# Turning 33 of 36 activation tiles by VectorE blocks and a DMA round trip instead of on TensorE

## The chip, the cores and the metric

The kernel runs on one core of one Trainium2 chip. The metric is the device time of one execution in microseconds (us). A core has five engines that run side by side, each in its own program order: TensorE (PE in the profile, with PEld for its weight loads), VectorE (DVE), ScalarE (ACT), GpSimd (POOL) and SyncE (SP), which here issues the DMA transfers. Engines hand work to each other by semaphores. TensorE writes to PSUM, all others work mostly in SBUF, and large arrays lie in HBM.

## The reference

First comes an attention with a feature map instead of a softmax: 8 batches, 8 heads, 576 positions, 64 channels. Then comes a gated feed-forward layer over the 4608 tokens, with 512 channels outside and 1024 inside.

```python
def phi(x):                       # 64 -> 2 x 128 features
    proj = x @ w_phi
    proj = proj - max(abs(proj), axis=-1)
    return concatenate([exp(proj), exp(-proj)], axis=-1)
q_p, k_p = phi(q), phi(k)
attn = (q_p @ (k_p.T @ v)) / (q_p @ sum(k_p, axis=seq) + 1e-6)
x = attn as (4608, 512)
h = x @ w_in                      # (4608, 1024)
sm = exp(h - max(h)) / (sum(exp(h - max(h))) + 1e-9)
solu = h * sm
ln = (solu - mean(solu)) / sqrt(var(solu) + 1e-6) * g_ln
out = ln @ w_out                  # (4608, 512)
```

All of it is float32. The kernel keeps that accuracy by splitting operands into a high and a low part and adding three products (high by high, high by low, low by high).

## The kernel before

**The work in pieces.** The attention runs over 16 units `u`, each a batch and half of its heads, in two halves `sub`. Keys are projected in five groups (`kp`), then reduced to their maximum, subtracted and exponentiated; a "visit" `V` sums the keys' features with the values on TensorE (`kvT`), and from the seventh visit on it also contains the previous half's numerators and denominators (`num`, `den`). Denominators go through a DMA that spreads them (`ds`, `db`). From unit 2 on, the sums `kv` are turned by VectorE in blocks of 32 by 32 (`kv_turn`), written to HBM (`kv_out`) and read back in four pieces (`kv_in`), which the plan names `kve`, `kvo` and `kvi`.

The feed-forward layer runs over 36 tiles `t` of 128 tokens, interleaved with the attention as their inputs come ready. For one tile: `moe_hi` and `moe_lo` split the input; `moe_h` multiplies it with `w_in` in two halves of 12 matmuls into a PSUM tile `h` of 128 by 1024; `moe_max`, `moe_exp` and `moe_u` on VectorE, ScalarE and VectorE make the gated activation `eu`; `moe_var` and `moe_scale` its scale; `moe_t` (line 1176) transposes `eu` on TensorE in two groups of four 128 by 128 blocks into a PSUM tile `uT`; `moe_uh` (line 1183) on ScalarE and `moe_ul` (line 1189) on VectorE split each group into the high part `uh` and the low part `ul`; `moe_o` (line 1193) multiplies these with `w_out` in two halves of 12 matmuls; `moe_oe` scales and `moe_od` stores.

**Buffers.** `SBUF_BUFS` (line 43) gives the number of buffers of each kind. `big` is a kind of 4 KB per partition: `eu`, `uh` and `ul` of a tile each take one, and the weights' preparation takes some at the start. `mo` is a pair of PSUM banks that `uT` and `o` share up to tile 30.

**The order.** Each piece is entered with `op(...)` into a `Plan`: engine, an estimated cost, what it comes after, which buffers it takes and which tiles it uses. `prioritize` (line 197) gives each piece a priority from two tables of numbers, and `order` (line 212) plays the plan through with the estimated costs and takes, on each engine, the piece that can start and has the best priority. The pieces are then issued in that order, and each engine keeps it: a piece that has to wait holds all behind it on the same engine. This includes SP, where a transfer that waits for its data holds the later ones. Every instruction is recorded through one helper (line 345), so groups in the profile are told apart by their tiles' names, not by their lines.

Of the kernel before, what the change touches and what calls it, by code (L numbers as in the profile page):

```python
# [8 lines left out]
F32 = mybir.dt.float32  # L9
# [11 lines left out]
P = 128  # L21
# [4 lines left out]
SWITCH, STICK, LINGER = 165.0, 400.0, 330.0  # L26
TILED = dict(visit=(1, 2), q_num=(1, 1), q_den=(2, 2))
# [4 lines left out]
JOIN, OWN = 6, 4  # L32
PORT = (
    "w_bits", "w_in_lo", "w_sum", "w_center", "w_out_lo", "k_lo", "z_add", "q_lo", "q_sub", "divide", "moe_lo",
)
# [4 lines left out]
TAIL_T = 31  # L40

# [3 lines left out]
    xa=1, xb=1, m2k=5, big=3, nm=2, sm=3, bst=2, mv=2, sa=2, sc=3,  # L45
# [5 lines left out]
WINDOW = 10240 / 3  # L51
START = dict(tensor=0.0, vector=950.0, scalar=4000.0, gpsimd=1750.0, sync=600.0)
LATENCY = {
    ("tensor", "vector"): 200, ("tensor", "scalar"): 200, ("scalar", "tensor"): 270, ("scalar", "vector"): 130,
    ("scalar", "gpsimd"): 160, ("vector", "tensor"): 260, ("vector", "scalar"): 130, ("vector", "gpsimd"): 200,
    ("gpsimd", "tensor"): 310, ("gpsimd", "scalar"): 120, ("gpsimd", "vector"): 150, ("vector", "vector"): 127,
    ("scalar", "scalar"): 143, ("gpsimd", "gpsimd"): 100, ("tensor", "tensor"): 60,
}

BASE = (
# [4 lines left out]
)  # L67
OFFSET = (
# [47 lines left out]
)  # L116


def act(n, psum=False, operands=0):
    return n / 1.2 + (51 if psum else 93) + 93 * operands  # L120


def dve(n):
    return (n + 65) / 0.96

# [16 lines left out]

class Plan:


    def __init__(self, bufs):
        self.ops, self.index, self.bufs = [], {}, dict(bufs)

    def op(self, name, engine, cost, prio, fn, args=(), after=(), alloc=(), tiles=(), early=None):
# [5 lines left out]
                 port=fn.__name__ in PORT, early=early or {})  # L155
        )

    @staticmethod
    def lat(a, b):
        if a == "start":  # L160
            return 0.0
# [1139 lines left out]
```

## Time and profile before

| | before |
|---|---|
| three runs | 774.5, 776.04, 776.7 us; median 776.04 |
| span of the profiled execution | 771.7 us (the profile shows no time outside of its span) |
| TensorE busy | 747.6 us, 97% of the span, 4935 matmuls |
| VectorE, ScalarE, GpSimd busy | 498.0, 384.1, 471.0 us |
| DMA | 75.35 MB in 99968 packets |

The span goes from the first to the last instruction. A run's time contains a little more than that, so a span is compared with a span and a median with a median. A row of a group reads: line, engine, operation, what it writes from what it reads, shapes, count, then busy us in total, mean ns of one, and the idle time of that engine just before, with what ended it. A row of the chain of waits reads: start us, duration us, engine or queue, tile, count; each piece is what released the next.

### The profile page before, as it was taken

Reading aid. Unit: us, or ns where it says so; the run is one execution under the profiler, and the core shown is the slowest. Engines: PE = TensorE matmul, PEld = TensorE weight load, DVE = VectorE, ACT = ScalarE, POOL = GpSimd, SP = SyncE. Lnnn points to the kernel's source line nnn. Section 1 sums busy time; section 2 is a strip of 40 time slices with the busy share of each in tenths; the row PEclk is TensorE's granted clock in tenths of the full one; section 3 lists DMA queues with packets and bytes.
Section 4 is the critical chain, followed back from the end, with each engine's and each line's share of the span. In section 5 each row is a group of like instructions: output and inputs, shape, how many; then the busy total and the mean of one; then the engine's idle time right before and its main releaser. Section 6 shows DMA issues by size and latency. Waiting matters only on the chain.

```text
span 771.7 us, 13472 instructions
## 1 busy us (share of the span) xinstructions
PE 747.6 (97%) x4935; PEld 564.6 (73%) x4935; DVE 498.0 (65%) x861; ACT 384.1 (50%) x750; POOL 471.0 (61%) x507
## 2 busy tenths in 40 slices
PE   5889999999999999999999999999999999999997
PEld 3566577777776777777777777778777777788885
DVE  4987896867568575766767658568377574435342
ACT  3776665465545455555546455545446354223221
POOL 1154799688957768694959786946849573422110
PEclk8899999999999999999999999999999999999999
DMA  7754432344333142524343433423323212110000
GB/s 237 291 177 134 110 106 66 92 135 139 84 111 94 54 128 75 136 75 120 104 110 113 132 92 98 122 67 101 84 71 102 68 35 62 40 44 27 14 24 31
DMA packets 99968, 75.35 MB, mean 98 GB/s; under 512 B 56128, under 2 KB 90432, under 8 KB 99392
## 3 DMA queue, kind: packets, MB, share of 16 engines
q1 hardware_dynamic: 99904, 74.50, 33.2%
q8 instruction: 39, 0.64, 0.3%
q14 instruction: 25, 0.20, 0.1%
HBM read 59.38 MB, written 15.09 MB: 96 GB/s over the span
## 4 chain that ended last, share of the span: by engine, by line
PE 93%; DVE 3%; DMA 1%; ACT 1%; SPq 1%; issue 1%; POOL 0%; ACTq 0%; POOLq 0%
PE o L345 26%; PE h L345 26%; PE kvT L345 11%; PE num L345 8%; PE pjk L345 6%; PE uT L345 4%; PE den L345 4%; PE pq L345 4%; DVE w L345 1%; PE pjq L345 1%; PE dT L345 1%; SPq L345 1%; DMA rawk<-in_k 1%; DVE cmp L345 0%; DVE m L345 0%
## 5 line engine op out<-in xcount | busy, mean ns | idle before, releaser
L345 PE MATMUL o<-w_out_h,uh 128*128 128x512 f32 x288 | 115.7, 402 | 0.5 <-DVE ul L345 0.5
L345 PE MATMUL o<-w_out_l,uh 128*128 128x512 f32 x288 | 114.1, 396 | 0.0
L345 PE MATMUL o<-w_out_h,ul 128*128 128x512 f32 x288 | 114.0, 396 | 0.0
L345 POOL TENSOR_TENSOR zacc<-zacc,ek 128x512 f32<-128x512 f32 (+1 forms) x78 | 100.7, 1291 | 19.2 <-ACT ek L345 13.3
L345 ACT ACTIVATE ek<-dk 128x512 f32<-128x512 f32 (+1 forms) x160 | 88.4, 582 | 42.9 <-DVE dk L345 42.6
L345 PE MATMUL h<-win_h,mxh 128*128 128x512 f32 x288 | 92.9, 404 | 0.0
L345 PE MATMUL h<-win_h,mxl 128*128 128x512 f32 x288 | 90.7, 396 | 0.0
L345 PE MATMUL h<-win_l,mxh 128*128 128x512 f32 x288 | 90.7, 396 | 0.0
L345 DVE TENSOR_REDUCE nm<-h 128x1 f32<-128x1024 f32 x36 | 43.9, 1220 | 63.4 <-PE h L345 63.3
L345 ACT ACTIVATE fq<-pT 128x576 f32<-128x576 f32 x104 | 68.9, 677 | 28.2 <-DVE pT L345 12.3
L345 ACT CAST uh<-uT 128x512 fp32r<-128x512 f32 x72 | 41.4, 585 | 83.6 <-PE uT L345 56.3
L345 POOL TENSOR_TENSOR blk<-blk,mcol 128x1152 f32<-128x1152 f32 x26 | 55.5, 2135 | 36.5 <-ACT mcol L345 36.3
L345 ACT ACTIVATE eu<-h,nm 128x1024 f32<-128x1024 f32 x36 | 40.2, 1117 | 68.9 <-DVE nm L345 62.1
L345 POOL TENSOR_TENSOR hq<-rawq,hq 64x1152 fp32r<-64x1152 f32 x26 | 69.1, 2658 | 7.2 <-ACT hq L345 4.9
L345 DVE TENSOR_TENSOR ul<-uT,uh 128x512 fp32r<-128x512 f32 x72 | 47.9, 676 | 37.4 <-ACT uh L345 37.3
L345 PE MATMUL num<-fq,kvf 128*64 128x288 f32 x512 | 69.3, 412 | 0.0
L345 DVE TENSOR_REDUCE m<-pjk 128x4 f32<-128x512 f32 (+1 forms) x80 | 48.8, 626 | 27.1 <-PE pjk L345 26.6
L345 PE MATMUL kvT<-ek,rawv 128*64 128x256 f32 x512 | 64.5, 383 | 1.7 <-ACT ek L345 1.7
L345 DVE TENSOR_TENSOR eu<-h,eu 128x1024 f32<-128x1024 f32 x36 | 43.9, 1218 | 34.0 <-ACT eu L345 34.0
L345 PEld LDWEIGHTS h<-win_h,mxl 128*128 128x128 f32 x288 | 54.3, 189 | 13.1
L345 PEld LDWEIGHTS o<-w_out_h,ul 128*128 128x128 f32 x288 | 54.2, 188 | 13.2
L345 PEld LDWEIGHTS h<-win_l,mxh 128*128 128x128 f32 x288 | 54.2, 188 | 13.1
(107 smaller groups left out, 1568.2 us busy)
## 6 DMA issues: line engine op xcount, KB each, us to landing
rawq<-in_q SPq DMA_DIRECT2D x26, 576.0 KB, 4.3
rb<-d SPq DMA_DIRECT2D x64, 144.0 KB, 3.3
out<-os SPq DMA_DIRECT2D x36, 256.0 KB, 2.0
rawk<-in_k SPq DMA_DIRECT2D x64, 128.0 KB, 2.8
rawv<-in_v SPq DMA_DIRECT2D x64, 128.0 KB, 2.3
dk<-kvs SPq DMA_DIRECT2D x28, 192.0 KB, 1.9
kvf<-dk SPq DMA_DIRECT2D x112, 48.0 KB, 2.5
wraw<-in_w_in SPq DMA_DIRECT2D x4, 1024.0 KB, 5.7
```

What stands on the lines that cost most here:

```text
L345: return self.tc.keep_in_program_order(method(*args, **kwargs))
```

## The change

Tiles 0 to 32 (`TURN_PE = 33`) no longer use `moe_t`. VectorE turns `eu` in 32 by 32 blocks into a buffer `B` (`moe_turn`); SP writes `B` to HBM in one transfer of 512 KB (`moe_bout`) and reads it back in four of 128 KB, one for each quarter of the partitions (`moe_bin`), so that features stand on partitions; ScalarE makes the high part in one copy of 1024 columns (`moe_uhs`) and VectorE the low part in one subtraction (`moe_uls`), both from SBUF. Tiles 33, 34 and 35 keep the old way.

There are eight `big` buffers instead of three; a changed tile takes five over its life (`eu`, `B`, `uT`, `uh`, `ul`). All eight prepared pieces of weights use `big`, where the last one used another kind. The two tables of priorities and the planner that plays the plan through are gone. In their place stands `SEQUENCE`, one table with the place of each of the 2827 pieces, and `order` only walks through it and hands out buffers. The relative order of the pieces that both kernels have differs too: on TensorE 65 of 474 common pieces stand at the same place among them, and none is moved by more than 19 places. The SBUF reserved for DMA descriptors that software writes is set to 2048 bytes.

```diff
+TURN_PE = 33
-    xa=1, xb=1, m2k=5, big=3, nm=2, sm=3, bst=2, mv=2, sa=2, sc=3,
+    xa=1, xb=1, m2k=5, big=8, nm=2, sm=3, bst=2, mv=2, sa=2, sc=3,
...
-BASE = (
...
-OFFSET = (
...
+SEQUENCE = (
+    3, 95, 0, 2, 136, 102, 132, 7, 97, 105, 140, 98, 133, 99, 88, 89, 106, 103, 107, 137, 117, 134, 135, 8, 144,
...
     def order(self):
...
+        for i in SEQUENCE:
+            o = self.ops[i]
+            assert written.issuperset(o["after"]), o["name"]
+            written.add(o["name"])
             for tag, t in o["alloc"]:
+                slot[t] = free[tag].pop(0)
+            for t in tiles[i]:
+                pending[t] -= 1
+                if not pending[t]:
+                    free[tag_of[t]].append(slot[t])
+        return [self.ops[i] for i in SEQUENCE]
...
-    w_tag = ("big", "big", "big", "big", "big", "big", "big", "e")
+    w_tag = ("big",) * 8
...
+    def moe_turn(t):
+        M["B", t] = sb("big", [P, 4, 8, 32], name="ub")
+        nc.vector.transpose(
+            out=M["B", t].rearrange("p b k j -> p k b j"),
+            in_=M["e", t].rearrange("p (k b i) -> p k b i", k=8, b=4),
+        )
+
+    def moe_bout(t):
+        M["du", t] = dram.tile([P, 4, 256], F32, tag="du", name="du", bufs=40)
+        nc.sync.dma_start(out=M["du", t], in_=M["B", t].rearrange("p b k j -> p b (k j)"))
+
+    def moe_bin(t, b):
+        if b == 0:
+            M["uT", t] = sb("big", [P, 4, 8, 32], name="uTs")
+        src = M["du", t].rearrange("(a i) b x -> i a b x", a=4)
+        nc.sync.dma_start(
+            out=M["uT", t][32 * b : 32 * b + 32].rearrange("p a k j -> p a (k j)"), in_=src[:, :, b, :]
+        )
+
+    def moe_uhs(t):
+        M["uh", t] = sb("big", [P, 8, P], F32R, "uhs")
+        M["turned", t] = M["uT", t].rearrange("p a k j -> p k a j")
+        nc.scalar.copy(out=M["uh", t].rearrange("p k (a j) -> p k a j", a=4), in_=M["turned", t])
+
+    def moe_uls(t):
+        M["ul", t] = sb("big", [P, 8, P], F32R, "uls")
+        full, hi, lo = M["turned", t], M["uh", t], M["ul", t]
+        hi, lo = (x.rearrange("p k (a j) -> p k a j", a=4) for x in (hi, lo))
+        hi_lo_sub(nc.vector, lo, full, hi)
+
...
-        for i in range(2):
+        by_dma = t < TURN_PE
+        if by_dma:
+            op(n("tb"), "vector", 1265, z + 8, moe_turn, (t,), [n("u")], [("big", n("B"))], [n("e")])
+            op(n("bo"), "sync", dma(4 * P * DF), z + 9, moe_bout, (t,), [n("tb")], (), [n("B")])
+            for b in range(4):
+                op(n("bi", b), "sync", (560, 440), z + 9.5, moe_bin, (t, b), [n("bi", b - 1) if b else n("bo")],
+                   () if b else [("big", n("uT"))], [n("uT")])
+            op(n("uh", 0), "scalar", act(DF), z + 11, moe_uhs, (t,), [n("bi", b) for b in range(4)],
+               [("big", n("uh"))], [n("uT")])
+            op(n("ul", 0), "vector", dve(DF), z + 12, moe_uls, (t,), [n("uh", 0)], [("big", n("ul"))], [n("uT"), n("uh")])
+        for i in range(0 if by_dma else 2):
...
-               [n("ul", hf)] + ([n("o", 0)] if hf else [("wol", f) for f in range(8)]),
+               [n("ul", 0 if by_dma else hf)] + ([n("o", 0)] if hf else [("wol", f) for f in range(8)]),
...
-    nc = bacc.Bacc("TRN2", target_bir_lowering=False, num_devices=1)
+    nc = bacc.Bacc("TRN2", target_bir_lowering=False, num_devices=1, dynamic_dma_scratch_size=2048)
```

More of the change, by code (lines that the diff above doesn't have):

```diff
@@ L25 @@
 EPS = 1e-6
-SWITCH, STICK, LINGER = 165.0, 400.0, 330.0
-TILED = dict(visit=(1, 2), q_num=(1, 1), q_den=(2, 2))
 K_PLAIN = (0, 1, 2)
@@ L31 @@
 KV_PE = (0, 1)
[L32 to L35, printed above, removed]
+SWITCH = 165.0
+JOIN = 6
 PJ_TAGS = ("mo", "h", "mo", "mo", "h")
@@ L49 @@
 NVZ = 2
[L51 to L58, printed above, removed]
-BASE = (
[4 rows of a table removed]
-)
-OFFSET = (
[47 rows of a table removed]
+SEQUENCE = (
[148 rows of a table added]
 )
@@ L153, in op @@
             dict(name=name, engine=engine, cost=cost, prio=prio, fn=fn, args=args, after=list(after),
-                 alloc=list(alloc), tiles=list(tiles), mode=TILED.get(fn.__name__, (0, 0)),
-                 port=fn.__name__ in PORT, early=early or {})
-        )
[L158 to L161, printed above, removed]
-        if a == "sync":
-            return 1150.0 if b == "tensor" else 910.0
-        return LATENCY.get((a, b), 150.0)
-    def dep_lat(self, a, b):
-        if a["engine"] == b["engine"] == "sync" and a["name"][:2] == b["name"][:2]:
-            return -1e9
-        return self.lat(a["engine"], b["engine"]) - a["early"].get(b["name"], 0.0)
@@ L171, in pe_end @@
-    @staticmethod
-    def pe_end(columns, t, cost):
-        rest = 2.4 * cost
-        while rest > 1e-6:
-            w = int(t / WINDOW)
-            rate = 2.4 if columns.get(w - 1, 0.0) >= 3060 else 1.2
-            n = min(rest, rate * ((w + 1) * WINDOW - t) + 1e-6)
-            columns[w] = columns.get(w, 0.0) + n
-            rest -= n
-            t += n / rate
-        return t
-    @staticmethod
-    def promote(ops, left, done, queue, head, free, ready):
-        def fits(i):
-            tags = [tag for tag, _ in ops[i]["alloc"]]
-            return tags and all(len(free[tag]) >= tags.count(tag) for tag in tags)
-        waiting = [i for e in ENGINES for i in ready[e] if fits(i)]
-        i = min(waiting, key=lambda i: (ops[i]["prio"], i))
-        for tag in {tag for tag, _ in ops[i]["alloc"]}:
-            rest = queue[tag][head[tag] :]
-            queue[tag][head[tag] :] = [x for x in rest if x[1] == i] + [x for x in rest if x[1] != i]
@@ L197, in prioritize @@
-    def prioritize(self):
-        groups, kinds = {}, {}
-        for o in self.ops:
-            group, kind = self.place(o["name"])
-            o["prio"] = BASE[groups.setdefault(group, len(groups))] + OFFSET[kinds.setdefault(kind, len(kinds))]
-    @staticmethod
-    def place(name):
-        if isinstance(name, str) or isinstance(name[0], str) and name[0] != "moe":
-            return "w", (name, "")
-        if name[0] == "moe":
-            return name[:2], ("moe", *name[2:])
-        return name[0], (name[1:], min(name[0], OWN))
@@ L212, in order @@
-    def order(self):
-        ops = self.ops
-        n = len(ops)
-        preds = [[self.index[a] for a in o["after"]] for o in ops]
-        succs = [[] for _ in range(n)]
-        for i, p in enumerate(preds):
-            for a in p:
-                succs[a].append(i)
-        left = [len(p) for p in preds]
-        users, tag_of = {}, {}
-        for i, o in enumerate(ops):
-            for tag, t in o["alloc"]:
-                tag_of[t] = tag
-            for t in set(o["tiles"]) | {t for _, t in o["alloc"]}:
-                users.setdefault(t, []).append(i)
-        pending = {t: len(u) for t, u in users.items()}
-        tile_end = {}
-        free = {tag: [(0.0, "start", k) for k in range(c)] for tag, c in self.bufs.items()}
-        slot = {}
-        queue = {tag: [] for tag in self.bufs}
-        for i, o in enumerate(ops):
-            for tag, t in o["alloc"]:
-                queue[tag].append((o["prio"], i, t))
-        for q in queue.values():
-            q.sort()
-        head = {tag: 0 for tag in self.bufs}
-        engine_free = dict(START)
-        done = [None] * n
-        ready = {e: [] for e in ENGINES}
-        for i in range(n):
-            if not left[i]:
-                ready[ops[i]["engine"]].append(i)
-        sequence = []
-        dma_free = 0.0
-        dma_done = [0.0] * 8
-        columns = {}
-        mode = 0
-        port = {"vector": (-1.0, -1), "gpsimd": (-1.0, -1)}
-        while len(sequence) < n:
-            best = None
-            for e in ENGINES:
-                cand = []
-                for i in ready[e]:
-                    t = engine_free[e]
-                    if e == "sync":
-                        t = max(t, dma_done[-8] + 910.0)
-                    for a in preds[i]:
-                        t = max(t, done[a] + self.dep_lat(ops[a], ops[i]))
-                    ok = True
-                    want = {}
-                    for tag, _ in ops[i]["alloc"]:
-                        want[tag] = want.get(tag, 0) + 1
-                    for tag, k in want.items():
-                        h = head[tag]
-                        mine = [x[1] for x in queue[tag][h : h + k]]
-                        if mine != [i] * k or len(free[tag]) < k:
-                            ok = False
-                            break
-                        f = sorted(free[tag])[k - 1]
-                        t = max(t, f[0] + self.lat(f[1], e))
-                    if ok:
-                        cand.append((t, ops[i]["prio"], i))
-                if not cand:
-                    continue
-                t0 = min(c[0] for c in cand)
-                same = lambda i: e != "tensor" or ops[i]["mode"][0] == mode
-                lim = max(t0, engine_free[e]) + 1e-6
-                pick = min(
-                    (c for c in cand if c[0] <= lim + (LINGER if e == "tensor" and 0 < ops[c[2]]["mode"][0] == mode else 0)),
-                    key=lambda c: (c[1] + (0 if same(c[2]) else STICK), c[2]),
-                )
-                if best is None or (pick[0], pick[1]) < (best[0], best[1]):
-                    best = (pick[0], pick[1], pick[2], e)
-            if best is None:
-                self.promote(ops, left, done, queue, head, free, ready)
-                continue
-            t, _, i, e = best
-            o = ops[i]
-            for tag, tl in o["alloc"]:
-                f = min(free[tag])
-                free[tag].remove(f)
-                slot[tl] = f[2]
-                head[tag] += 1
-            if e == "sync":
-                hold, transfer = o["cost"]
-                hold += 180 if len(dma_done) < 15 else 40 if len(dma_done) < 22 else 0
-                engine_free[e] = t + hold
-                dma_free = done[i] = max(t + hold + 625, dma_free) + transfer
-                dma_done.append(done[i])
-            elif e == "tensor":
-                engine_free[e] = done[i] = self.pe_end(columns, t, o["cost"] + SWITCH * (o["mode"][0] != mode))
-                mode = o["mode"][1]
-            else:
-                end = t + o["cost"]
-                if o["port"]:
-                    other = "gpsimd" if e == "vector" else "vector"
-                    busy, j = port[other]
-                    shared = min(o["cost"], max(0.0, busy - t))
-                    if shared > 0:
-                        end += shared
-                        engine_free[other] += shared
-                        done[j] += shared
-                        port[other] = (busy + shared, j)
-                    port[e] = (end, i)
-                engine_free[e] = done[i] = end
-            ready[e].remove(i)
-            sequence.append((t, i))
-            for s_ in succs[i]:
-                left[s_] -= 1
-                if not left[s_]:
-                    ready[ops[s_]["engine"]].append(s_)
-            for tl in set(o["tiles"]) | {x for _, x in o["alloc"]}:
-                pending[tl] -= 1
-                prev = tile_end.get(tl, (0.0, e))
-                tile_end[tl] = max(prev, (done[i], e))
-                if not pending[tl]:
-                    free[tag_of[tl]].append((*tile_end[tl], slot[tl]))
-        self.slot = slot
-        self.length = max(done)
-        self.start = {ops[i]["name"]: t for t, i in sequence}
-        return [ops[i] for _, i in sequence]
@@ new lines, in op @@
+                 alloc=list(alloc), tiles=list(tiles), early=early or {})
+        )
+    def order(self):
+        assert sorted(SEQUENCE) == list(range(len(self.ops)))
+        tiles = [list(dict.fromkeys([*o["tiles"], *(t for _, t in o["alloc"])])) for o in self.ops]
+        tag_of = {t: tag for o in self.ops for tag, t in o["alloc"]}
+        pending = {}
+        for t in (t for ts in tiles for t in ts):
+            pending[t] = pending.get(t, 0) + 1
+        free = {tag: list(range(c)) for tag, c in self.bufs.items()}
+        self.slot = slot = {}
+        written = set()
+        for i in SEQUENCE:
+            o = self.ops[i]
+            assert written.issuperset(o["after"]), o["name"]
+            written.add(o["name"])
+            for tag, t in o["alloc"]:
+                slot[t] = free[tag].pop(0)
[4 more added lines that the diff above has]
+        return [self.ops[i] for i in SEQUENCE]
@@ L1254, in linear_attention_then_moe @@
         op(n("od"), "sync", dma(4 * P * DM), z + 19, moe_od, (t,), [n("oe")], (), [n("os")])
-    plan.prioritize()
     for o in plan.order():
```

198 rows, old and new, of tables (BASE, OFFSET, SEQUENCE) are left out of this document.

## The prediction

> **What bounds the kernel now.** The page comes first: engine totals, slices, chain of waits.
>
> ```profile
> span 771.7 us, 13472 instructions
> PE 747.6 (97%) x4935; PEld 564.6 (73%) x4935; DVE 498.0 (65%) x861; ACT 384.1 (50%) x750; POOL 471.0 (61%) x507
> ...
> PEclk8899999999999999999999999999999999999999
> ...
> q1 hardware_dynamic: 99904, 74.50, 33.2%
> ...
> PE 93%; DVE 3%; DMA 1%; ACT 1%; SPq 1%; issue 1%; POOL 0%; ACTq 0%; POOLq 0%
> ```
>
> TensorE is busy 747.6 of 771.7 us and is 93% of the chain that ended last. Since a busy PE need not be a full one, the busy time by stage comes second, and the chain in a stretch of the middle third.
>
> ```profile
> 0.00:100.00 100.00, 83.87 (x722) 56.24 (x723) 76.45 (x112) 63.29 (x130) 42.01 (x40) 0.95 0.59 185
> 100.00:640.00 540.00, 537.25 (x3585) 409.29 (x3584) 368.81 (x673) 283.52 (x554) 397.76 (x413) 1.00 0.34 97
> 640.00:760.00 120.00, 119.97 (x604) 94.21 (x602) 51.37 (x75) 35.19 (x64) 30.92 (x55) 1.00 0.11 33
> ```
> ```profile
> 444.69 2.09 PE num L345 x16
> 446.78 2.51 PE kvT L345 x28
> 449.29 0.97 PE den L345 x16
> 450.26 0.59 PE uT L345 x4
> ...
> 450.96 0.71 PE pjk L345 x6
> 451.67 0.44 PE uT L345 x4
> ...
> 452.80 0.27 PE pq L345 x2
> 453.07 2.81 PE h L345 x12
> ```
>
> The columns of the first are the stretch, then busy us (instructions) of PE, PEld, DVE, ACT, POOL, then clock, DMA share, GB/s. PE idles 16.1 us before 100 us, 2.8 in the next 540, nothing after that up to the end; the clock is full from 100 us on. In the chain every piece starts where the last one ends: from 100 us on the time is the sum of PE's pieces, and a piece taken out of them is time saved if nothing arrives late. The very end is the exception:
>
> ```profile
> 753.90 5.65 PE o L345 x24
> ...
> 759.63 0.69 ACT os L345
> ...
> 760.82 0.70 DVE ul L345
> ...
> 761.57 5.90 PE o L345 x24
> ```
>
> PE ends a tile at 759.55 and waits for ScalarE and VectorE until 761.57: 2.0 us.
>
> **The change part by part.**
>
> *TensorE: two groups of four transposes leave 33 of 36 tiles, 66 groups.* A group on the chain is 0.44 us; it is 0.59 behind `den`, where the 0.15 belongs to the return from narrow to full tiles and falls to whatever comes next. 66 x 0.44 = 29.0 us. All 288 matmuls are these:
>
> ```profile
> L345 PE MATMUL uT<-ident,eu 128*128 128x128 f32 x288 | 43.6, 278 | 0.4 <-ACT os L345 0.4
> L345 DVE TENSOR_TENSOR eu<-h,eu 128x1024 f32<-128x1024 f32 x36 | 43.9, 1218 | 34.0 <-ACT eu L345 34.0
> L345 DVE TENSOR_TENSOR ul<-uT,uh 128x512 fp32r<-128x512 f32 x72 | 47.9, 676 | 37.4 <-ACT uh L345 37.3
> L345 DVE STREAM_TRANSPOSE pT<-blk 128x288 f32<-128x288 f32 x104 | 41.5, 442 | 1.9 <-POOL blk L345 1.8
> L345 DVE TENSOR_TENSOR w<-w,cms 128x512 f32<-128x512 f32 x8 | 9.0, 1167 | 1.0 <-ACT cms L345 1.0
> L345 ACT ACTIVATE eu<-h,nm 128x1024 f32<-128x1024 f32 x36 | 40.2, 1117 | 68.9 <-DVE nm L345 62.1
> L345 ACT CAST uh<-uT 128x512 fp32r<-128x512 f32 x72 | 41.4, 585 | 83.6 <-PE uT L345 56.3
> L345 ACT CAST win_h<-w 128x1024 fp32r<-128x1024 f32 x4 | 4.2, 1062 | 2.9 <-DVE w L345 2.9
> ```
>
> I take 29.0. The upper end counts their modelled ends as well: 43.6 x 66/72 = 40, which no start-to-start spacing bears out; with the 0.15 in half of the groups it is 31, my bound.
>
> *VectorE.* A 1024-wide block transpose is not in the trace. Below, it is a 1024-wide pass, 1.22 us; above, in proportion to 288 columns, 0.442 x 1024/288 = 1.57. I take 1.25, as the 288-wide row has a start-up of its own. The low half becomes one 1024-wide subtraction from two SBUF tiles instead of two 512-wide ones from PSUM (1.35 us a tile). The only such subtraction here, `w<-w,cms`, took 1167 ns for 512 columns where the PSUM form took 676. So it is 1.22 to 2.33; I take 1.7. Per tile VectorE gains 1.25 + 1.7 - 1.35 = 1.6 us, 53 in all: 551 of about 744, 74%. Over the middle, 27 tiles' 43 us in a stretch some 25 us shorter, it goes from 368.8/540 = 68% to 80%. This hides under PE; without that cover it would cost 53 us.
>
> *ScalarE* has one copy of 1024 columns from SBUF, 1.06 us, for two of 0.585: nothing gained or lost.
>
> *SP and the DMAs.* Five transfers a tile, 165 in all. The same round trip exists already for `kvs`:
>
> ```profile
> L345 SPq DMA_DIRECT2D dk<-kvs x28: 325/326/333, 84.3 to 652.5; - x28
> L345 SPq DMA_DIRECT2D kvf<-dk x112: 563/615/1343, 87.0 to 656.4; - x112
> ...
> dk<-kvs SPq DMA_DIRECT2D x28, 192.0 KB, 1.9
> kvf<-dk SPq DMA_DIRECT2D x112, 48.0 KB, 2.5
> rawk<-in_k SPq DMA_DIRECT2D x64, 128.0 KB, 2.8
> rawq<-in_q SPq DMA_DIRECT2D x26, 576.0 KB, 4.3
> ...
> SPq L345 <- ACT os L345: 189.6, 30, 14.6
> ```
>
> Issue costs SP 0.33 + 4 x 0.615 = 2.8 us a tile, 92 in all. SP waits 190 us for `os` alone while PE loses nothing, so the time is there. What counts is the order: behind a write waiting for its transpose stand loads of k and v, `kvo`, `ds` and `db`, and behind a `kvo` may stand this tile's reads. The bytes add at most 33 x 1 MB to 74.5, so the share of 33.2% goes to about 50%.
>
> *The latency that must be covered.* From the last `h` matmul of a tile: maximum 1.22, exponential 1.12 + 0.2, product 1.22, hand-overs 0.3: 4.1. Transpose 1.25. Write: issue 0.33, landing between 1.9 (192 KB) and 4.3 (576 KB); for 512 KB written without reading HBM I take 2.6. Four reads: 2.5 to issue, 2.8 for the last to land. Copy 1.06, subtraction 1.7, hand-overs 0.3. Sum 16.6 us.
>
> Against it stands what the new table puts on PE between a tile's last `h` and its first `o`, by the chain's durations (projection groups 0.71 and 0.27; a visit 2.09 + 2.51 + 0.97 + 0.15 = 5.72; halves of `h` and `o` 2.81). For tile 20: three halves 8.43, one visit 5.72, three k groups 2.13, three q groups 0.81, two small transposes 0.22: 17.3. The others: tiles 3 and 15 18.2, 2 18.9, 30 19.9, 14 20.3, 18 20.8, 5 21.0, 4 21.3, 0 22.6, 6 23.2, 17 23.3, the remaining 21 of the 33 between 26 and 41. All exceed 16.6. But on SP tiles 20 and 3 have `kvo` of a visit that ends 9.9 us in ahead of their reads: 9.9 + 0.2 + the block transpose 0.6 + issue 0.33 + 2.5 + 2.8 + 1.06 + 1.7 + 0.3 = 19.4. They are late by 2.1 and 1.2, so 3.3 us of new waiting. Bounds: 0 if copies come at once; and at most, a VectorE operation that waits out a POOL operation. That happens here:
>
> ```profile
> 241.57 2.65 POOL L345 TENSOR_TENSOR hq<-rawq,hq 64x1152 fp32r<-64x1152 f32 x1
> ...
> 241.78 2.47 DVE L345 TENSOR_SCALAR cmp<-dE 128x9 f32<-128x9 f32 x1
> ```
>
> A nine-column operation lasted until POOL's ended. With 2.65 more the latency is 19.3, and 22.1 for tiles 20 and 3: 4.8 + 3.9 + 1.1 + 0.4 = 10.2 us, my upper bound. [...]
>
> *The order table and the eight buffers.* The tail's new order ends with the halves of tiles 33 and 27 in turn; tile 33 has 20.5 us of cover with its transposes on PE, tile 27 35.0. So the 2.0 us at 759.55 go. PSUM banks `mo` no longer hold `uT`: a freedom that I price at nothing, as PE doesn't idle. Planning code and priorities cost the chip nothing. The smaller descriptor scratch is free: the 74.5 MB of the queue quoted are issued by SP, and no row of the page has a DMA from POOL. The start is reordered too: 16.1 us of idle are at stake before 100 us. VectorE has the same work there, 76.5 of 100 us, so I take 0, with -8 (half of the idle) to +8 (the same again) as bounds.
>
> *Sum.* 771.7 - 29.0 - 2.0 + 3.3 = 744.0 us of span. The profiled execution shows no time beside its span; the runs' median of 776.04 is 4.3 above it. 744.0 + 4.3 = 748.3, forecast 748. Lowest: 771.7 - 31 - 2 - 8 + 4.3 = 735. Highest: 771.7 - 29 + 10.2 + 8 + 4.3 = 765.
>
> **The rivals.**
>
> *The round trip is too long: slower.* Every tile's `o` waits for latency less cover. With 23 us the shortfalls are 5.7, 4.8, 4.8, 4.1, 3.1, 2.7, 2.2, 2.0, 1.7, 0.4: 31.5, which eats the 31 saved; that is the point from which it decides. With 25 they sum to 55: 748.3 - 3.3 + 55 = 800. For it: latency in one in-order SP queue adds up, and DVE at 80%, in order, makes queues. Against: `kvf` covers the same path, its last read issued 3.9 us behind its last write (652.5 to 656.4), and 23 needs 6 us more than the rows give. [...]
>
> *Covers bite by half.* Latency of 20 to 21.5 us, from queues on VectorE and ScalarE: at 21.5, shortfalls 4.2 + 3.3 + 3.3 + 2.6 + 1.6 + 1.2 + 0.7 + 0.5 + 0.2 = 17.6, time 748.3 - 3.3 + 17.6 = 763. For: tile 20 has some 16 us of VectorE work queued within its 17.3.
>
> *The start gets shorter as well.* Half of the idle before 100 us goes: 740. For: a new order with more buffers; against: VectorE's same 76 us.
>
> *Nothing comes of it.* The freed time returns as waits on VectorE in the attention part: 776. Against: 2.8 us idle in 540 with the tighter `uT` hand-overs.
>
> **How the numbers follow.** The forecast case (741 to 755) 0.60; covers by half (756 to 770) 0.14; shorter start (734 to 740) 0.13; nothing 0.05; slower 0.08. 0.3% is 2.3 us, about what a measurement of this kernel tells from no change. Faster: 0.60 + 0.14 + 0.13 = 0.87; same 0.05; slower 0.08. The range 735 to 766 leaves out the last two, the edge of the second and third: under 2 in 10.
>
> **What would show it.** Right: 24 `uT` matmuls left; PE busy about 747.6 - 29 = 718; idle before `o` a few us, at tiles 20 and 3; transposes near 1.25 us; subtractions spread between 1.2 and 3.9 us. Wrong: `o` waiting for `ul` at many tiles; reads landing above 4 us; PE idle before 100 us far from 16; a clock below 1.00 in the middle.

## The result, and the profile after

The changed kernel takes 742.26 us in the median of four runs (739.48 to 742.67), the kernel before 776.37 on the same chip (774.5 to 777.57). The ratio is 0.9559, with a 95% interval from 0.9534 to 0.9585. In every run of both kernels whose span is on record the time is 1.8 to 2.1 us above that span. One run of an experiment below, in the chip's slower state, is left out of its median and ratio.

The page of the changed kernel, its totals and the row of SyncE's queue:

```profile
span 740.4 us, 13275 instructions
PE 716.5 (97%) x4671; PEld 533.0 (72%) x4671; DVE 545.4 (74%) x861; ACT 377.1 (51%) x717; POOL 485.2 (66%) x507
...
q1 hardware_dynamic: 123664, 109.11, 51.7%
```
```profile
0.00:100.00 100.00, 89.41 (x782) 62.28 (x782) 86.47 (x129) 66.93 (x141) 42.55 (x41) 1.00 0.63 191
100.00:616.00 516.00, 507.08 (x3312) 377.40 (x3312) 398.30 (x654) 271.01 (x511) 406.91 (x405) 1.00 0.55 154
616.00:736.00 120.00, 119.43 (x578) 93.18 (x577) 60.58 (x79) 38.47 (x64) 35.72 (x62) 1.00 0.30 92
```

The second fence is the busy time by stage, in the columns of the prediction. 264 matmuls are gone, 33 tiles of eight. TensorE's idle time has hardly changed in total, 23.9 us against 24.1, but it has moved: 10.6 us before 100 us (16.1 in the kernel before), 9.5 between there and 736 us (2.8 between 100 and 640), 3.8 at the end (5.2).

The times at which tile 0's maximum starts, in the timelines of before and then of after, show the gain at the start. Behind them stands the end of the changed kernel, where the last `o` product runs without a break and only ScalarE's scaling and the store follow:

```profile
106.87 1.22 DVE L345 TENSOR_REDUCE nm<-h 128x1 f32<-128x1024 f32 x1 [0.35 <-PE h L345]
```
```profile
93.07 1.23 DVE L273 TENSOR_REDUCE nm<-h 128x1 f32<-128x1024 f32 x1 [0.48 <-PE h L273]
...
736.70 0.69 ACT L273 ACTIVATE os<-o,sc 128x512 f32<-128x512 f32 x1 [2.12 <-PE o L273]
```

The ledger of the span, all from such rows. TensorE's busy time at full clock was 747.6 x 0.993 = 742.4 us and is 716.5 x 0.999 = 715.8 (the factors are the mean granted clocks of the two executions, rounded to three places and averaged over idle stretches too, so that this term and the next are good to about 1 us): 26.6 us of work are gone. The clock gave another 4.5, nearly all of it at the start, where before had 0.95 in the first 100 us and after has 1.00. Idle time: 5.5 less at the start, 6.7 more in the middle, 1.4 less at the end. The sum is -26.6 - 4.5 - 5.5 + 6.7 - 1.4 = -31.3, the difference of the spans.

The new operations and what they touch, in the groups of after (busy us, mean ns, idle before), and the two new transfers with KB and us to landing:

```profile
L273 DVE STREAM_TRANSPOSE ub<-eu 128x1024 f32<-128x1024 f32 x33 | 40.7, 1232 | 0.7
L273 DVE TENSOR_TENSOR uls<-uTs,uhs 128x1024 fp32r<-128x1024 f32 x33 | 56.6, 1714 | 20.5 <-ACT uhs L273 19.5 <-DMA rawk<-in_k 0.8
L273 DVE TENSOR_SCALAR cmp<-dE 128x9 f32<-128x9 f32 x32 | 17.5, 546 | 1.1
...
L273 POOL TENSOR_TENSOR zacc<-zacc,ek 128x512 f32<-128x512 f32 (+1 forms) x78 | 107.6, 1379 | 27.4 <-ACT ek L273 23.2 <-POOL zacc L273 0.2
```
```profile
du<-ub SPq DMA_DIRECT2D x33, 512.0 KB, 2.9
uTs<-du SPq DMA_DIRECT2D x132, 128.0 KB, 3.2
```

And what TensorE waited for between 100 and 616 us (us in total, times, longest):

```profile
PE pq L273 <- DVE mt L273: 2.5, 4, 1.0
PE o L273 <- DVE uls L273: 1.7, 2, 1.4
PE pjk L273 <- DVE dk L273: 1.4, 1, 1.4
PE pjk L273 <- ACT E L273: 0.9, 1, 0.9
```

The turned tiles themselves account for 1.7 us of these, and for 0.6 us later on. TensorE's timeline has the three waits of `o` for a low part:

```profile
120.27 0.50 PE L273 MATMUL o<-w_out_h,uls 128*128 128x512 f32 x1 [1.36 <-DVE uls L273]
...
525.41 0.50 PE L273 MATMUL o<-w_out_h,uls 128*128 128x512 f32 x1 [0.34 <-DVE uls L273]
...
655.66 0.50 PE L273 MATMUL o<-w_out_h,uls 128*128 128x512 f32 x1 [0.57 <-DVE uls L273]
```

By the order of the table these are tiles 0, 25 and 30, and the subtractions that they waited for had taken 2.88, 3.71 and 2.38 us. Most other waits of this stage are hand-overs of the attention. One instruction shows a mechanism that can stand behind both: the low part's subtraction has a least duration of 1.18 us and a longest of 3.71 (the row gives least, median and longest ns), and the longest one, tile 25's, is this in the timeline of after:

```profile
L273 DVE TENSOR_TENSOR uls<-uTs,uhs x33: 1182/1252/3710, 117.3 to 724.4; 128x1024 fp32r<-128x1024 f32 x33
```
```profile
521.58 2.69 POOL L273 TENSOR_TENSOR hq<-rawq,hq 64x1152 fp32r<-64x1152 f32 x1
521.64 3.71 DVE L273 TENSOR_TENSOR uls<-uTs,uhs 128x1024 fp32r<-128x1024 f32 x1 [1.50 <-ACT uhs L273]
```

GpSimd's instruction started 0.06 us earlier and ended at 524.27; the subtraction ended 1.08 us after that, as if it had only begun then.

### The profile page after: what moved, and what is told of

It reads as the page before. It is cut to its first block, busy times and chain, and to the rows that moved or that the text cites. A ratio compares the mean times of both kernels' runs of the same rounds, so it can differ in the third digit from the quotient of the medians.

```text
span 740.4 us, 13275 instructions
## 1 busy us (share of the span) xinstructions
PE 716.5 (97%) x4671; PEld 533.0 (72%) x4671; DVE 545.4 (74%) x861; ACT 377.1 (51%) x717; POOL 485.2 (66%) x507
## 3 DMA queue, kind: packets, MB, share of 16 engines
q1 hardware_dynamic: 123664, 109.11, 51.7%
## 5 line engine op out<-in xcount | busy, mean ns | idle before, releaser
L273 POOL TENSOR_TENSOR zacc<-zacc,ek 128x512 f32<-128x512 f32 (+1 forms) x78 | 107.6, 1379 | 27.4 <-ACT ek L273 23.2
L273 ACT ACTIVATE ek<-dk 128x512 f32<-128x512 f32 (+1 forms) x160 | 90.0, 585 | 51.0 <-DVE dk L273 47.8
L273 PE MATMUL o<-w_out_h,uls 128*128 128x512 f32 x264 | 104.9, 397 | 2.3 <-DVE uls L273 2.3
L273 PE MATMUL o<-w_out_h,uhs 128*128 128x512 f32 x264 | 105.3, 399 | 0.0
L273 PE MATMUL o<-w_out_l,uhs 128*128 128x512 f32 x264 | 104.3, 395 | 0.0
L273 DVE TENSOR_TENSOR uls<-uTs,uhs 128x1024 fp32r<-128x1024 f32 x33 | 56.6, 1714 | 20.5 <-ACT uhs L273 19.5
L273 POOL TENSOR_TENSOR xa<-E,rb 128x576 f32<-128x576 f32 (+1 forms) x32 | 30.4, 953 | 58.0 <-DMA rb<-d 36.4
L273 PEld LDWEIGHTS o<-w_out_h,uls 128*128 128x128 f32 x264 | 49.6, 188 | 16.6 <-DVE uls L273 4.9
L273 POOL TENSOR_TENSOR xl<-rawk,xh 128x256 fp32r<-128x256 f32 (+1 forms) x65 | 46.2, 714 | 21.6 <-ACT xh L273 20.9
```

Source lines behind the costliest of these rows:

```text
L273: return self.tc.keep_in_program_order(method(*args, **kwargs))
```

## The experiments

The kernel before ran beside each kernel; its medians went from 773.6 to 776.4 over the chips. So kernels are set against the changed one by ratios to before, 0.9559 for the changed kernel, where 0.001 is 0.77 us.

### Whose is the shorter start?

Three runs. First, the pieces ahead of tile 0's `h` that both orders share are put into the old relative order, in the first 395 places of the table alone, which begins so:

```diff
 SEQUENCE = (
-    3, 95, 0, 2, 136, 102, 132, 7, 97, 105, 140, 98, 133, 99, 88, 89, 106, 103, 107, 137, 117, 134, 135, 8, 144,
+    136, 2, 0, 103, 3, 95, 132, 7, 4, 96, 118, 5, 102, 97, 209, 89, 323, 133, 88, 98, 99, 100, 137, 134, 101, 140, 135,
...
```

> The changed kernel, but the pieces ahead of the first tile's h product that both orders share stand in the relative order of the kernel before (one piece is put off until what it needs is there). Theory (the order of the start's pieces is what saved 9.3 us there): tile 0 comes at 102 to 107 us and the time is 742.3 + 9.3 = about 751 (748 to 754). Rival (the buffers, or TensorE's clock in the first 100 us, saved it): tile 0 at 93 to 95 us, time 741 to 744.

Measured: 755.51 us, ratio 0.9744 (0.9714 to 0.9774), 14 us more than the changed kernel. Timeline and first stage:

```profile
107.30 1.22 DVE L265 TENSOR_REDUCE nm<-h 128x1 f32<-128x1024 f32 x1
```
```profile
0.00:100.00 100.00, 82.23 (x718) 55.63 (x719) 72.37 (x109) 59.58 (x122) 31.35 (x34) 0.97 0.57 179
```

Tile 0 is back at 107 us with eight buffers and the DMA turn in place, idle before 100 us is 17.8 us, and VectorE has done 72.4 us of work by then instead of 86.5. The order makes the start, given the eight buffers, which both runs have; whether it would fit into three was not tested. The run is still 20 us below the kernel before: that much is the turn with the rest of the new order. The size of the start is 14, not 9; a start and a rest that weren't laid out for each other may cost something of their own, which this run can't separate.

Second, the kernel before with the eight buffers, the smaller descriptor scratch and its own planner:

```diff
-    xa=1, xb=1, m2k=5, big=3, nm=2, sm=3, bst=2, mv=2, sa=2, sc=3,
+    xa=1, xb=1, m2k=5, big=8, nm=2, sm=3, bst=2, mv=2, sa=2, sc=3,
...
-    w_tag = ("big", "big", "big", "big", "big", "big", "big", "e")
+    w_tag = ("big",) * 8
...
```

> The kernel before with the eight 4 KB buffers (the weights' fourth and eighth kind of load uses them too) and the smaller DMA scratch, and nothing else; its own planner orders it. Theory (order, not room): tile 0 stays at about 107 us and the time at 774 to 779. Rival (weights that load earlier shorten the start): tile 0 at 93 to 98 us, time 764 to 770.

Measured: 830.01 us, ratio 1.0716 (1.0682 to 1.0749), and tile 0 later than ever:

```profile
119.03 1.22 DVE L345 TENSOR_REDUCE nm<-h 128x1 f32<-128x1024 f32 x1 [2.31 <-PE h L345]
```

Neither expectation held. More room alone doesn't shorten the start; the planner, whose tables of numbers belong to three buffers, made another and worse order of the whole from it. That confounds the run: it shows only that buffers without a fitting order bring nothing.

Third, the new table, but all tiles turned on TensorE:

```diff
-        by_dma = t < TURN_PE
+        by_dma = t < 0
```

(with the 66 groups put into the table behind their tiles' `h` products).

> The changed kernel's order table and eight buffers, but all 36 tiles turned on TensorE again; the turning pieces stand in the table at the same distance behind a tile's last h product as before. Theory (the shorter start comes from the order and the buffers, the 29.0 us from the turns): the group that carries normalisation of tile 0 still comes at about 93 us (107 before, 93 after), TensorE's busy time is back at about 745, and the time is 742.3 + 29.0 = 771, plus what my own placing of 66 groups costs, at most some 10 us: 769 to 781. Rival (the start is shorter because the turn left TensorE and PSUM): tile 0 is back at about 107 us and the time is at or over 776, 776 to 790.

Measured: 880.89 us, ratio 1.137 (1.1336 to 1.1403). Timeline and page:

```profile
92.06 1.22 DVE L261 TENSOR_REDUCE nm<-h 128x1 f32<-128x1024 f32 x1
```
```profile
PE 780.6 (89%) x4935; PEld 578.5 (66%) x4935; DVE 505.0 (57%) x861; ACT 379.6 (43%) x750; POOL 470.5 (54%) x507
```

On the start the theory held: tile 0 comes at 92 us without any DMA turn. On the total both were too low by about 100 us. My placing left TensorE 97.7 of 878.3 us idle, and the same 4935 matmuls that took 747.6 us before took 780.6. So this run doesn't price the turns; a table of places can't be changed by 66 groups with a simple rule.

### What does the cover of the table carry?

The changed kernel's DMA turn in the old order: a tile's new pieces go in at their least latency behind its last `h`, and its `o` stays where it was. The table begins so:

```diff
 SEQUENCE = (
-    3, 95, 0, 2, 136, 102, 132, 7, 97, 105, 140, 98, 133, 99, 88, 89, 106, 103, 107, 137, 117, 134, 135, 8, 144,
+    136, 2, 0, 1, 103, 3, 95, 132, 7, 4, 96, 118, 5, 102, 97, 209, 89, 323, 133, 88, 98, 99, 100, 137, 134, 101, 140,
...
```

> The changed kernel's DMA turn for the same 33 tiles, but the order of the kernel before, with the new pieces put in at their least latency behind the tile's last h product and nothing of the rest moved: a tile's first o product stands where it stood. Theory (the gain hangs on the cover that the table builds, a latency of 17.5 us or more from last h product to low part): TensorE waits in front of most turned tiles' o products for the low part, 2 to 3 us a tile in the mean, 60 to 90 us in all on 771.7 - 29.0 = 742.7: 800 to 835 us. Rival (the order matters little, other products fill in): 745 to 755 us.

Measured: 951.67 us, ratio 1.2297 (1.2233 to 1.2361). TensorE's waits over the whole span:

```profile
PE o L265 <- ACT uhs L265: 76.9, 17, 9.1
PE pq L265 <- DVE dk L265: 22.8, 6, 8.5
PE pq L265 <- ACT mcol L265: 17.3, 2, 9.2
PE o L265 <- DVE uls L265: 9.1, 11, 2.0
```

The waits of `o` sum to 86.0 us, inside the 60 to 90 that the covers gave. What I had left out came on top: TensorE is idle for 167.4 of 946.9 us, as late tiles make the attention's pieces late, and the same 4671 matmuls took 779.5 us instead of 716.5. One wait shows why. TensorE's timeline of this run, then the clock (last but two columns) in the stretches behind the wait:

```profile
304.14 0.80 PE L265 MATMUL o<-w_out_h,uhs 128*128 128x512 f32 x1 [8.52 <-ACT uhs L265]
304.74 0.63 PE L265 MATMUL o<-w_out_l,uhs 128*128 128x512 f32 x1
305.40 0.80 PE L265 MATMUL o<-w_out_h,uls 128*128 128x512 f32 x1
...
308.17 0.40 PE L265 MATMUL o<-w_out_h,uhs 128*128 128x512 f32 x1
308.41 0.39 PE L265 MATMUL o<-w_out_l,uhs 128*128 128x512 f32 x1
```
```profile
304.00:306.00 2.00, 1.82 (x4) 1.00 (x4) 1.88 (x3) 0.61 (x2) 0.00 (x0) 0.50 0.00 0
306.00:308.00 2.00, 2.00 (x7) 1.57 (x6) 1.97 (x7) 0.00 (x0) 0.00 (x0) 0.58 0.00 0
308.00:310.00 2.00, 2.00 (x10) 1.63 (x9) 0.41 (x2) 0.00 (x0) 0.00 (x0) 1.00 0.20 44
```

After 8.52 us without work the granted clock is 0.50; matmuls start 0.60 to 0.66 us apart instead of 0.24, until it is 1.00 again by 308 us, some 4 us after work resumes. A wait is paid twice. What a shorter wait does to the clock these rows don't show.

### Do the last three tiles gain too?

```diff
-TURN_PE = 33
+TURN_PE = 36
```

> The changed kernel with the last three tiles turned by VectorE and the DMA round trip too, their new pieces put in at the latency of the others and the rest of the table as it is. Theory (each group taken off TensorE is worth 0.44 us as long as the o product stands more than 17.5 us of TensorE time behind the last h product; here it is 19.6, 37 and 29 us for tiles 33, 34 and 35): 742.3 - 6 x 0.44 = 739.7 us, 738.5 to 741. Rival (the tail has no cover to spare): a wait for the low part of 2 to 6 us ahead of one of the three o products, 742 to 747 us.

Measured: 747.72 us, ratio 0.9647 (0.9622 to 0.9673), 7 us more than the changed kernel. TensorE's waits from 600 us on:

```profile
PE h L265 <- DVE eu L265: 3.7, 2, 3.2
PE o L265 <- ACT os L265: 1.3, 1, 1.3
```

The rival's sign holds, its size nearly (742 to 747), but not its place: no `o` waits for a low part. An `h` product waits for the PSUM tile that `eu`'s product on VectorE still reads. Placed like this, the remaining tiles are better off on TensorE. Not all of the 7 us need be theirs: the two tables are alike up to the last 120 or so places, and yet the clock in the first 100 us of this execution is 0.98, for 1.00 in the changed kernel's. That is some 2 us of work, and the run with its additions in PSUM, further down, shows the same 0.98 with its start unchanged in order.

This run can't price the six groups. TensorE's busy time at full clock is 717.0 x 0.995 = 713.4 us, for 715.8 in the changed kernel, but runs below with all of the changed kernel's 4671 matmuls come to 713.2 (713.9 x 0.999) and 716.5 (717.9 x 0.998).

### Is it VectorE that the middle pays for?

Less of it: the low part without 15/16 of its columns (the slice keeps eight columns in each of eight blocks, 64 of 1024, not the 32 that I expected), and the third product reads the high part in its place. The second pair of lines does that:

```diff
-        hi_lo_sub(nc.vector, lo, full, hi)
+        hi_lo_sub(nc.vector, lo[:, :, 0, :8], full[:, :, 0, :8], hi[:, :, 0, :8])
...
-            nc.tensor.matmul(o, lhsT=ul[:, fc, :], rhs=w_out_part("h", fc), start=False, stop=(fc == 7))
+            nc.tensor.matmul(o, lhsT=(uh if t < TURN_PE else ul)[:, fc, :], rhs=w_out_part("h", fc), start=False, stop=(fc == 7))
```

> The changed kernel with 32 of the 1024 columns of each turned tile's low part subtracted, the rest of the low part left out; the third product reads the high part in its place, so TensorE does the same work. VectorE has some 33 x 1.6 = 53 us less to do. Theory (the 11 us that TensorE waits behind tile 0, 9 more than before, are VectorE's load): these waits fall to 2 to 5 us, time 734 to 739 us. Rival (they come from the planned order and the latencies, with VectorE idle a quarter of the time): 741 to 743 us.

More of it: the subtraction twice.

```diff
         hi_lo_sub(nc.vector, lo, full, hi)
+        hi_lo_sub(nc.vector, lo, full, hi)
```

> The changed kernel with each turned tile's low part made twice over: VectorE has 33 x 1.7 = 56.6 us more, about 602 of 742 us, and a tile's o product can start 1.7 us later. Theory (VectorE's load is what the middle waits for, and has little to spare): 750 to 765 us, with waits for VectorE ahead of the attention's products and of o. Rival (the table has slack of 27 us in the median from last h product to low part, and VectorE is idle for a quarter): at most 3 us more, 742 to 745 us.

Measured: 733.68 us with less (ratio 0.9473, 0.9452 to 0.9495), 790.75 with more (1.0206, 1.0163 to 1.0248), so by the ratios 6.7 us below and 50 above the changed kernel. Both go the theory's way, the second far beyond it. In the run with more, page and waits:

```profile
PE 730.0 (93%) x4671; PEld 538.6 (68%) x4671; DVE 600.3 (76%) x894; ACT 378.0 (48%) x717; POOL 507.9 (65%) x507
```
```profile
PE o L273 <- DVE uls L273: 21.8, 15, 3.6
PE pq L273 <- DVE mt L273: 7.7, 4, 3.2
```

54.9 us more of VectorE cost 46 us of span, though VectorE is idle for a quarter of it: 32.6 us of new idle time on TensorE and 13.5 of longer busy time. 15 `o` products now wait for their low part. Taking VectorE's time away saves a quarter of it, adding costs nearly all. That suggests that the table holds each product about as early as these durations allow. The cost is not VectorE's time alone, though: each low part also comes later, and GpSimd's busy time grew as well, from 485.2 to 507.9 us.

The middle stage of the run with less:

```profile
100.00:616.00 516.00, 512.36 (x3348) 384.64 (x3348) 381.75 (x660) 276.51 (x522) 398.78 (x409) 1.00 0.56 155
```

TensorE idles 3.6 us there, for 8.9 in the changed kernel. But the few columns left should take a fraction of a microsecond:

```profile
L273 DVE TENSOR_TENSOR uls<-uTs,uhs x33: 180/227/2681, 116.3 to 715.7; 128x64 fp32r<-128x64 f32 x33
```
```profile
515.21 2.68 POOL L273 TENSOR_TENSOR hq<-rawq,hq 64x1152 fp32r<-64x1152 f32 x1
515.29 2.68 DVE L273 TENSOR_TENSOR uls<-uTs,uhs 128x64 fp32r<-128x64 f32 x1 [1.51 <-ACT uhs L273]
```

The work is 0.18 us, the longest takes 2.68 and ends 0.08 us behind GpSimd's instruction. So VectorE had lost only 27.9 us (545.4 less 517.5), not 53. That led to the next runs.

### Work, or waiting for GpSimd?

The low part is replaced by a copy with a single input of the same size, first of the turned tile, then, since that one no longer waits for ScalarE's rounding, of the high part:

```diff
-        hi_lo_sub(nc.vector, lo, full, hi)
+        nc.vector.tensor_reduce(out=lo, in_=full.unsqueeze(4), axis=AX.X, op=ALU.max)
```
```diff
-        hi_lo_sub(nc.vector, lo, full, hi)
+        nc.vector.tensor_reduce(out=lo, in_=hi.bitcast(F32).unsqueeze(4), axis=AX.X, op=ALU.max)
```

> The changed kernel, but the turned tile's third operand is made by an instruction of VectorE that reads one tensor of SBUF (a copy of the turned tile, rounded) in place of the subtraction that reads two; so the low part is left out and something else stands in its place, with 128x1024 elements as before. Theory (the subtraction's mean of 1.71 us against its least of 1.18 us is waiting for GpSimd to end an instruction that reads SBUF): each of the 33 takes 1.1 to 1.25 us, GpSimd's 78 running sums go back from 1.38 to about 1.29 us each, VectorE has some 17 us less, and by the 0.31 us of time per us of VectorE that leaving out the low part gave (8.6 for 27.9) the time is 737 us (735 to 740). Rival (it is VectorE's work, not the waiting for GpSimd): 741 to 743.5 us.

> As the kernel whose low part is a copy with one input, but the copy reads the rounded high part, so that it waits for ScalarE as the subtraction does (the low part is left out, a second copy of the high part stands in its place). Theory (it was the subtraction's waiting for GpSimd that cost some 8 us): 33 copies of 1.20 us, 733 to 737 us. Rival (that kernel gained because its copy no longer waited for ScalarE's rounding, 1.05 us a tile): 739 to 743 us.

Measured: 734.07 us (ratio 0.9483, 0.9463 to 0.9504) and 735.8 us (0.9508, 0.949 to 0.9525). The instructions of the two, and GpSimd's sums in the second:

```profile
L273 DVE TENSOR_REDUCE uls<-uTs x33: 1170/1204/1222, 114.7 to 714.6; 128x1024 fp32r<-128x1024 f32 x33
```
```profile
L273 DVE TENSOR_REDUCE uls<-uhs x33: 1167/1206/1223, 114.6 to 718.0; 128x1024 fp32r<-128x1024 f32 x33
```
```profile
L273 POOL TENSOR_TENSOR zacc<-zacc,ek 128x512 f32<-128x512 f32 (+1 forms) x78 | 100.8, 1292 | 26.9 <-ACT ek L273 22.7
```

```profile
100.00:616.00 516.00, 509.24 (x3331) 383.01 (x3330) 386.15 (x658) 274.47 (x519) 395.10 (x407) 1.00 0.55 155
```

The last row is the second's middle stage. With one input from SBUF none of 66 instructions takes more than 1.223 us, where the subtraction reached 3.71; and GpSimd's sums fall from 1.379 to 1.292 us, so GpSimd's instructions get longer beside the subtraction too. In time the second copy, the clean one, is worth 4 us by the ratios, with intervals some 2.5 us wide on each side. The theory's 733 to 737 us hold by the median; by the ratio (0.9508 of the 776.4 of the changed kernel's chip is 738) it stands between theory and rival. So the waiting for GpSimd costs about 4 us, give or take 2.5. The first copy's further 2 us lie inside the intervals.

Two inputs are not the whole of it. The attention's nine-column additions read one tensor of SBUF and write to SBUF, as the copies do, yet in the changed kernel they take 173 to 1772 ns. The one that starts at 570.51 us there lasts 1.49 us, to 0.04 us behind the end of GpSimd's `hq` (569.29 + 2.67). Why these wait and the copies don't, no run shows. Their output can lie in PSUM as well, in columns that the bank has free:

```diff
-        c = work.tile([P, HC // 32], F32, tag="cmp", bufs=8, name="cmp")
+        c = st["den", sub][:, HC : HC + HC // 32]
```

> The changed kernel, but the 32 small additions to the attention's denominators write their nine columns into the free columns of the denominators' PSUM bank, not to SBUF; nothing is left out. Theory (in the kernel as changed these 128x9 additions take 173 to 1772 ns, 546 in the mean, because they too wait until GpSimd's instruction ends; with one side in PSUM they don't): 200 to 260 ns each, 10 us less of VectorE, 742.3 - 0.31 x 10 = 739 us (737.5 to 741). Rival (they stand where VectorE has slack): 741.5 to 743.5 us.

> The kernel before, with the additions to the denominators written into the PSUM bank, as the run on the kernel as changed had them (nothing left out). There they take 453 ns in the mean; they should take 178, 8.8 us less of VectorE. Theory (VectorE's lost time costs only since the change made its queue tight; before, TensorE waits 2.2 us behind tile 0): 0 to 2 us less than the kernel before, ratio 0.997 to 1.000. Rival (the additions' wait was on the path all along): the same 6 us as on the changed kernel, ratio 0.990 to 0.993.

Measured on the changed kernel: 736.04 us (735.72 to 738.56), ratio 0.9512 (0.9493 to 0.953), 3.6 us below it by the ratios. This one beats both kernels. On the kernel before: 770.96 us, ratio 0.9965 (0.9951 to 0.9978), 2.7 us. The additions of the first, and its middle stage:

```profile
L273 DVE TENSOR_SCALAR den<-dE x32: 174/177/179, 38.1 to 641.1; 128x9 f32<-128x9 f32 x32
```
```profile
100.00:616.00 516.00, 508.60 (x3321) 379.51 (x3320) 393.79 (x658) 271.74 (x513) 410.50 (x405) 1.00 0.55 155
```

With one side in PSUM none waits: 177 ns instead of 546. On the kernel before the ratio stands just below the theory's 0.997 to 1.000, with an interval that reaches into it, and well above the rival's 0.990 to 0.993. So the additions cost something before the change too, but 2.7 us, not 6. Set beside the 3.6 us on the changed kernel, whose interval is some 2.5 us wide on each side, it leaves open whether the change made them dearer.

Last, shorter pieces to wait for:

```diff
-        hi_lo_sub(nc.gpsimd, hq[D:], st["rq", sub][D:], hq[D:])
+        for j in range(2):
+            for c in range(2):
+                x = hq[D:, j, c * HC : (c + 1) * HC]
+                hi_lo_sub(nc.gpsimd, x, st["rq", sub][D:, j, c * HC : (c + 1) * HC], x)
...
+        for i in range(4):
+            x = blk[:, 9 * i : 9 * i + 9]
+            nc.gpsimd.tensor_tensor(out=x, in0=x, in1=mc[:, 9 * i : 9 * i + 9], op=ALU.subtract)
```

> The changed kernel with the denominators' additions in PSUM, and GpSimd's two longest instructions of the attention cut into four each (the low part of q, 2.70 us, and the blocks less their maxima, 2.13 us), so that VectorE's subtraction waits behind pieces of 0.5 to 0.7 us; nothing is left out. Theory (the wait is as long as the rest of GpSimd's instruction): the 33 subtractions fall from 1.71 to about 1.55 us in the mean, time 734 to 735.5 us against 736.0 without the cut. [...]

Measured: 743.57 us, ratio 0.9608 (0.9592 to 0.9624), 7 us more than without the cut.

```profile
L273 DVE TENSOR_TENSOR uls<-uTs,uhs 128x1024 fp32r<-128x1024 f32 x33 | 50.3, 1523 | 20.4 <-ACT uhs L273 20.2
...
L273 POOL TENSOR_TENSOR hq<-rawq,hq 64x288 fp32r<-64x288 f32 x104 | 84.3, 842 | 5.9 <-ACT hq L273 3.5 <-POOL blk L273 0.8
L273 POOL TENSOR_TENSOR blk<-blk,mcol 128x288 f32<-128x288 f32 x104 | 69.6, 700 | 1.1 <-ACT mcol L273 0.8
```

The subtractions do what was expected, 1.52 us. But the time is 8 us above the theory's 734 to 735.5: four pieces of 0.842 us stand for one of 2.67 (in the run without the cut), so a further piece costs 0.23 us, and GpSimd is busy 25.6 us longer (515.2 for 489.6).

## Why the prediction was right, and where its steps were off

The forecast was 748, the result 742.26: the sign, the stage and the order of size came from the right reading, that TensorE's pieces set the time from 100 us on. That the sum came within 6 us is in part luck: the start alone was mis-sized by 10, and the turns, the end and the new waits, off by 6.4 together, went the other way. These are the terms (predicted span 744.0, measured 740.4; then what lies outside).

- **The turns, -29.0: 26.6 by the ledger.** That is 0.40 us a group, for 0.44 by the spacing in the chain. That a piece behind `den` takes longer holds in the changed kernel too: from its start to the next piece's a k group takes 0.81 us there, for 0.71 behind `h` or `o`, and a q group 0.37 for 0.26. The difference isn't clear of the spread: the runs with the same 4671 matmuls come to 713.2 to 716.5 us at full clock where their order is undisturbed, against 742.4 and 743.8 (746.8 x 0.996, with the additions in PSUM) for the 4935 of before, so 26 to 31 us. The size stands; no run takes the turns alone out of the change, as the one meant to do it left TensorE idle for 98 us. The upper bound was added up wrongly: 0.15 in half of the 66 groups is 5, which makes it 34, not 31, and the lowest time 732, not 735.
- **The end, -2.0:** the break at the last tile is gone; in idle time the end got 1.4 us shorter.
- **The start, 0: about -10.** This step failed. I read VectorE's 76.5 us of work in the first 100 us as work that any order has to do there. It was what that order had managed: the new one gets 86.5 us done by then. TensorE's idle time fell by 5.5 us, to 10.6, far from the 16 that the prediction expected, and the clock, 0.95 before, stayed at 1.00 (0.98 in two other executions with the same start, so some 2 us of this vary). The rival of a shorter start, which I gave 0.13, is what happened, on top of the main case; the run with the old start shows that the order does it.
- **The new waits, +3.3: +6.7.** The mechanism of this term failed too. Tiles 20 and 3, which I named as late behind a `kvo`, don't wait at all: their low parts were ready 17.5 and 18.7 us after their maximum had started, for the 19.4 forecast, and 17.5 is also the shortest of all 33, for 16.6. `o` waited 2.3 us for low parts in the whole span, at tiles 0, 25 and 30, each time behind a subtraction of 2.4 to 3.7 us. The rest came where I had not looked, at the attention's hand-overs on VectorE and GpSimd. Less VectorE time brings part of it back, in the run without most of the low part (3.6 us idle in this stage against 8.9) and in the one-input copies (5.1 and 6.8). That the subtraction would wait out GpSimd's operations stood in the prediction as a bound, and as a wait for a tile's own `o`; it is paid there in part, and otherwise in the queue behind it. The pair of rows that the prediction shows for it is of another operation, the nine-column addition with one input (2.47 us beside 2.65); that its wait goes with its output in PSUM, 177 ns for 546, was shown only later, by that run. Which of the remaining waits come from the order's own planning stays open.
- **Outside the span, +4.3: +1.9.** The profiled execution of before, at a span of 771.7, was a short one; its time would be 773.6 by the 1.9 us that other runs of this kernel show. I took the distance to the median for time outside of the span.
- **VectorE.** Transposes 1.232 us for 1.25, subtractions 1.714 for 1.7 (1.18 to 3.71 for 1.22 to 3.9), total 545.4 for 551; middle 398.30/516 = 77% for 80%. ScalarE came out 7.0 us lower, 377.1, for unchanged.
- **The DMA.** Write and reads landed after 2.9 and 3.2 us, for 2.6 and 2.8; the share of 51.7% is the 50 forecast.
- **The long round trip.** In the changed table it is covered. Without such a table the rival is real: in the old order `o` waits 86 us, and the whole comes to 952. The rival had the mechanism right and stopped at its first term, for a late tile also delays the attention and lowers the clock, to 0.918 in that run's mean.

## What to carry to other kernels

Where TensorE's pieces follow each other without a break, a removed piece is worth about its spacing in the chain (29.0 us predicted, 26 to 31 measured); then look for what it costs on the engines that take it over: here a quarter to nearly all of added or removed VectorE time counted although VectorE was idle for a quarter of the span. Before giving VectorE a new operation with two SBUF inputs, count what GpSimd runs beside it (the subtraction took 1.714 us in the mean, the copies with one input 1.20), and let one side lie in PSUM where that is free (the old subtractions of 512 columns from PSUM took 644 to 693 ns in all 72 cases, those of 1024 from SBUF 1.18 to 3.71 us). A start is a matter of order: busy time in it is what the old order managed, not what has to be done.

## What the hardware showed that I had not expected

A nine-column addition of VectorE takes up to 1.77 us beside GpSimd's work with both sides in SBUF, and 174 to 179 ns in all 32 cases with its output in PSUM. GpSimd's running sums take longer beside VectorE's two-input subtraction, 1.379 us in the mean, than beside the copy, 1.292. A cut of a GpSimd instruction costs 0.23 us for each further piece. And each us of new TensorE idle time brought 0.4 us of longer busy time with it: 13.5 for 32.6 in the run with the subtraction twice, 63 for 143.5 in the old order. Most of that is the lower clock: at the mean clocks of 0.987 and 0.918 the busy times would be 720.5 and 715.6 us at full clock, for 715.8 in the changed kernel.
